# A SwiGLU kernel: two adjacent x rows per partition in one load, and strided PSUM copies

## The chip, the cores and the metric

The kernel runs on one core of one Trainium2 chip. The metric is the device time of one execution in microseconds (us), taken as the median over several runs. Besides the timed runs there is one profiled execution, from which all views of the trace come.

## The reference

x has 2048 rows of 640 elements; w_gate and w_up are 640 x 1536, w_down is 1536 x 640; all are bf16.

```python
B, S, D, F = 1, 2048, 640, 1536

def reference(x, w_gate, w_up, w_down):
    g = _silu(x @ w_gate)
    u = x @ w_up
    return (g * u) @ w_down
```

## The kernel before

The rows of x are worked off in four blocks of 512 (`S_BLK`). Everything contracts over the partitions, so x is needed turned: `xT` holds x with the 640 inner elements as 5 slices (`KD`) of 128 partitions and the 2048 rows as columns. The weights stay in SBUF whole: `wg_sb` and `wu_sb` by 5 slices, `wd_sb` by 12 chunks (`KF`).

For each block and each of the 12 chunks of F, TensorE makes a gate tile `pg` and an up tile `pu` (5 matmuls each, 128 x 512, in `proj`, line 193), ScalarE (ACT) takes the silu of `pg` into `sg` (line 214), and VectorE (DVE) multiplies `sg` with `pu` into `aT` (line 215). Then the block's output is made: 12 matmuls for the last 128 output columns (`po_t`, line 261), and four groups of 12 for the first 512 (`po_a`, line 291), with copies to SBUF and stores. The last four rows of x are worked out apart, on VectorE, as sums of products over turned weights (`row_dots`, line 147), between its other work.

How x comes into `xT`: rows 0 to 255 are loaded as they are, into `x_sb`, in two loads of 128 rows, one issued by SP and one by ACT (line 86), and turned by TensorE. Columns 256 to 511, 512 to 1023, 1024 to 1535 and 1536 to 2047 are turned by the DMA itself on the way in (`turn_x`, line 105), all issued by SP. The first of these is issued ahead of the up weights, the second behind all weight loads (`wd_sb`, line 125, is the last of them), the other two after block 0's outputs. Each gate slice `kd` of the first four chunks (`EARLY`) has its own load (line 115): slice 1 goes by ACT's queue, the others by SP's.

The start is written out in `head()`. TensorE runs 18 warm-up matmuls on a constant tile (`pw`, line 176), then for each of the two 128-row chunks of `x_sb` five transposes into PSUM tiles `pt` (line 185). Two copies per chunk carry them to `xT` (line 190): ACT takes slices 0 and 1, DVE slices 2 to 4. Then come 44 gate matmuls for the first four chunks (`proj_step`, line 193): slice 0 in two halves of 128 columns (4 + 4 matmuls), slices 1 to 4 over columns 0 to 255 (16), and slices 0 to 4 over columns 256 to 511 (20). After them come 20 up matmuls.

The order on SP, DVE, PE and ACT is the order of the program (`keep_order`, in `head` for PE and ACT). Which instruction waits for which is worked out by the framework from the memory that each reads and writes: a write that overlaps an earlier write of the same tile waits for it.

Of the kernel before, what the change touches and what calls it, by code (L numbers as in the profile page):

```python
# [10 lines left out]
def _body(  # L11
# [8 lines left out]
    nc = tc.nc  # L20
    P = nc.NUM_PARTITIONS
# [8 lines left out]
    x2 = x.rearrange("b s d -> (b s) d")  # L30
    out2 = out.rearrange("b s d -> (b s) d")

    KD = D // P
    KF = F // P
    S_BLK = 512
    NSB = S // S_BLK
    SUB = S_BLK // P
    HALF = S_BLK // 2
# [18 lines left out]
    x_sb = consts.tile([P, HALF // P, D], bf16)  # L57
    xT = consts.tile([P, KD, S], bf16)
    wg_sb = consts.tile([P, KD, F], bf16)
# [10 lines left out]

    make_identity(nc, ident[:])

    x_v = x2.rearrange("(c p) d -> p c d", p=P)
    xt_v = x2.rearrange("s (kd p) -> s kd p", p=P)
    wg_v = w_gate.rearrange("(kd p) f -> p kd f", p=P)
    wu_v = w_up.rearrange("(kd p) f -> p kd f", p=P)
# [2 lines left out]
    def wslice(a, b):  # L79
        return slice(a * P, b * P)  # L80

    def load_w(eng, dst, src, a, b):
        eng.dma_start(out=dst[:, :, wslice(a, b)], in_=src[:, :, wslice(a, b)])

    def load_x(eng, c0, c1):
        eng.dma_start(out=x_sb[:, c0:c1, :], in_=x_v[:, c0:c1, :])  # L86

    def issue_order(a, b):
        tc.add_manual_dep(
# [8 lines left out]
    def keep_order(engine):  # L98

        traced = [i for i in nc.cur_bb.bb.instructions if i.engine == engine]  # L100
        for a, b in zip(traced, traced[1:]):
            issue_order(a, b)
# [5 lines left out]
    silu_first = consts.tile([P, 1], f32)  # L108
    nc.vector.memset(ones[:], 1.0)  # L109

    load_x(nc.sync, 0, 1)
    load_x(nc.scalar, 1, 2)
    for kd in range(KD):
        eng = nc.scalar if kd == 1 else nc.sync
        eng.dma_start(
            out=wg_sb[:, kd, wslice(0, EARLY)], in_=wg_v[:, kd, wslice(0, EARLY)]
        )
# [11 lines left out]
    def turn_w(dst, src, f0, f1):  # L129
# [7 lines left out]
        out=x_row[:],  # L137
        in_=x2[S - T : S, :].rearrange("t d -> (t d)").partition_broadcast(P),
# [35 lines left out]
    def warm(n):  # L174
        for _ in range(n):
            nc.tensor.matmul(  # L176
                pw[:, 0:P], lhsT=ones[:], rhs=ones[:], start=True, stop=True
            )

    def transpose_chunk(c, parts):  # L180
        c_sl = slice(c * P, (c + 1) * P)
        for copy, tag, k0, k1 in parts:
            pt = psum.tile([P, k1 - k0, P], bf16, tag=tag, name="pt")
            for kd in range(k0, k1):
                nc.tensor.transpose(  # L185
                    out=pt[:, kd - k0, :],
                    in_=x_sb[:, c, kd * P : (kd + 1) * P],
                    identity=ident[:],
                )
            copy(out=xT[:, k0:k1, c_sl], in_=pt[:])  # L190

    def proj_step(ps, w_sb, fc, sb, c0, c1, kd):
        nc.tensor.matmul(  # L193
            ps[:, c0:c1],
            lhsT=w_sb[:, kd, fc * P : (fc + 1) * P],
            rhs=xT[:, kd, sb * S_BLK + c0 : sb * S_BLK + c1],
            start=(kd == 0 and c0 in (0, HALF)),
            stop=(kd == KD - 1),
        )

    def proj(ps, w_sb, fc, sb, c0, c1):
        for kd in range(KD):
            proj_step(ps, w_sb, fc, sb, c0, c1, kd)
# [6 lines left out]
    def gate(pg, pu, sb, fc, n_s):  # L210

        s0 = sb * S_BLK
        sg = work.tile([P, S_BLK], f32, name="sg")
        nc.scalar.activation(sg[:, 0:n_s], pg[:, 0:n_s], ACT.Silu)  # L214
        nc.vector.tensor_tensor(  # L215
            out=aT[:, fc, s0 : s0 + n_s], in0=sg[:, 0:n_s], in1=pu[:, 0:n_s], op=ALU.mult
        )

    def head():
        dve, act = nc.vector.tensor_copy, nc.scalar.copy  # L220
        split = [(act, "po_a", 0, 2), (dve, "po_b", 2, KD)]
        pgs = [
            psum.tile([P, S_BLK], f32, tag="gu", name="pg", bufs=4)
            for _ in range(EARLY)
        ]
        warm(N_WARM)
        for c in range(HALF // P):
            transpose_chunk(c, split)

        steps = [(0, 0, P), (0, P, HALF)]  # L230
        steps += [(kd, 0, HALF) for kd in range(1, KD)]
        steps += [(kd, HALF, S_BLK) for kd in range(KD)]
        for kd, c0, c1 in steps:
            for fc in range(EARLY):
                proj_step(pgs[fc], wg_sb, fc, 0, c0, c1, kd)

        for fc in range(EARLY):
            pu = psum.tile([P, S_BLK], f32, tag=("po_a", "po_b")[fc % 2], name="pu")
            proj(pu, wu_sb, fc, 0, 0, S_BLK)
            gate(pgs[fc], pu, 0, fc, S_BLK)  # L240
        keep_order(mybir.EngineType.PE)
        keep_order(mybir.EngineType.Activation)

    head()
    for sb in range(NSB):
        n_s = S_BLK if sb < NSB - 1 else S_BLK - T
# [13 lines left out]
        for kf in range(KF):  # L260
# [3 lines left out]
                rhs=aT[:, kf, sb * S_BLK : sb * S_BLK + n_t],  # L264
# [8 lines left out]
        for q in range(P // Q):  # L273
            nc.scalar.dma_start(
                out=out2[
                    sb * S_BLK : sb * S_BLK + n_t, DA + q * Q : DA + (q + 1) * Q
                ].rearrange("(i r) c -> r i c", r=Q),
                in_=ot_q[q * Q : (q + 1) * Q, :].rearrange("r (i c) -> r i c", c=Q),
            )

        for j in range(SUB):
# [6 lines left out]
            for c0, c1, tag in cols:  # L288
                po = psum.tile([P, c1 - c0], f32, tag=tag, name="po_a")
                for kf in range(KF):  # L290
# [3 lines left out]
                        rhs=wd_sb[:, kf, c0:c1],  # L294
# [8 lines left out]
                eng = nc.sync if c1 < D else nc.scalar  # L303
# [82 lines left out]
def kernel(tc, *args):  # L386
    _body(tc, *args)
    tc.close()
    tc.compile()
    _trim(tc.nc)  # L390
# [30 lines left out]
```

## Time and profile before

| what | value |
|---|---|
| median of 3 runs | 163.31 us (163.09 to 163.35) |
| span of the profiled execution, first to last instruction | 161.8 us |
| TensorE (PE) busy | 159.4 us, 99% of the span |
| VectorE (DVE) busy | 111.0 us, 69% |
| ScalarE (ACT) busy | 42.6 us, 26% |
| DMA moved | 15.86 MB |
| granted TensorE clock | 1.000 |

For the profiled execution the trace gives its span alone; the median of the timed runs is 1.5 us longer than that span.

How to read the views: PE is TensorE's matmuls, PEld its weight loads, SP the engine that issues most transfers; SPq and ACTq are instructions that an engine's sequencer handles, such as the issue of a transfer. A tile stands under its name in the program. `x44` is a count. "Idle before" is the time for which an engine stood still ahead of an instruction, and the arrow names what ended it. The span is also cut into 40 equal slices of 4.0 us, with a digit for the busy tenths in each. A transfer has an issue (the time that the issuing sequencer spends on it) and a landing (when all its data are in).

### The profile page before, as it was taken

Reading aid. Unit: us, or ns where it says so; the run is one execution under the profiler, and the core shown is the slowest. Engines: PE = TensorE matmul, PEld = TensorE weight load, DVE = VectorE, ACT = ScalarE, POOL = GpSimd, SP = SyncE. Lnnn points to the kernel's source line nnn. Section 1 sums busy time; section 2 is a strip of 40 time slices with the busy share of each in tenths; the row PEclk is TensorE's granted clock in tenths of the full one; section 3 lists DMA queues with packets and bytes.
Section 4 is the critical chain, followed back from the end, with each engine's and each line's share of the span. In section 5 each row is a group of like instructions: output and inputs, shape, how many; then the busy total and the mean of one; then the engine's idle time right before and its main releaser. Section 6 shows DMA issues by size and latency. Waiting matters only on the chain.

```text
span 161.8 us, 2142 instructions
## 1 busy us (share of the span) xinstructions
PE 159.4 (99%) x808; PEld 77.6 (48%) x808; DVE 111.0 (69%) x250; ACT 42.6 (26%) x74; POOL 0.6 (0%) x6
## 2 busy tenths in 40 slices
PE   8999999999999999999999999999999999999995
PEld 7854444444444444444444444444444444445454
DVE  2034223599569999989919999979964999993001
ACT  5051222112222222211222322221214222222121
POOL 1000000000000000000000000000000000000000
PEclk9999999999999999999999999999999999999999
DMA  6999999934189999003110000000321000000312
GB/s 212 231 351 349 361 248 231 222 75 91 34 192 159 235 236 184 4 0 34 65 65 0 0 4 2 0 0 3 62 67 34 0 0 0 0 0 4 48 41 73
DMA packets 41961, 15.86 MB, mean 98 GB/s; under 512 B 33504, under 2 KB 41824, under 8 KB 41952
## 3 DMA queue, kind: packets, MB, share of 16 engines
q1 hardware_dynamic: 33584, 14.93, 37.0%
q10 hardware_dynamic: 8368, 0.80, 3.5%
q8 instruction: 6, 0.10, 0.3%
q14 instruction: 3, 0.02, 0.1%
HBM read 6.88 MB, written 2.62 MB: 59 GB/s over the span
## 4 chain that ended last, share of the span: by engine, by line
PE 97%; DMA 2%; SPq 0%; DVE 0%; issue 0%
PE pg L193 32%; PE pu L193 32%; PE po_a L291 26%; PE po_t L261 6%; DMA wg_sb<-in_w_gate_dram 2%; SPq L86 0%; DVE ot_b L302 0%
## 5 line engine op out<-in xcount | busy, mean ns | idle before, releaser
L193 PE MATMUL pg<-xT,wg_sb 128*128 128x512 bf16 (+3 forms) x264 | 59.8, 363 | 0.1
L193 PE MATMUL pu<-xT,wu_sb 128*128 128x512 bf16 (+1 forms) x240 | 59.1, 379 | 0.0
L215 DVE TENSOR_TENSOR aT<-sg,pu 128x512 bf16<-128x512 f32 (+1 forms) x48 | 32.7, 682 | 32.3 <-PE pu L193 32.3
L214 ACT ACTIVATE sg<-pg 128x512 f32<-128x512 f32 (+1 forms) x48 | 28.4, 597 | 71.2 <-PE pg L193 67.4
L291 PE MATMUL po_a<-wd_sb,aT 128*128 128x512 bf16 (+4 forms) x228 | 42.8, 348 | 0.0
L147 DVE SCALAR_TENSOR_TENSOR prod<-wgT,x_row 128x640 f32<-128x640 bf16 x48 | 39.4, 821 | 1.5 <-DMA wgT<-in_w_gate_dram 0.4
L147 DVE SCALAR_TENSOR_TENSOR prod<-wuT,x_row 128x640 f32<-128x640 bf16 x48 | 39.4, 821 | 1.0
L193 PEld LDWEIGHTS <-wg_sb 128*128 128x128 bf16 x264 | 25.9, 100 | 26.8 <-DMA wg_sb<-in_w_gate_dram 0.4
L193 PEld LDWEIGHTS <-wu_sb 128*128 128x128 bf16 x240 | 23.4, 98 | 28.1 <-DMA wu_sb<-in_w_up_dram 0.3
L291 PEld LDWEIGHTS <-aT 128*128 128x128 bf16 x228 | 20.8, 98 | 21.7
L300 ACT CAST ot<-po_a 128x512 bf16<-128x512 f32 (+2 forms) x17 | 9.5, 559 | 31.8 <-PE po_a L291 20.2
L261 PE MATMUL po_t<-aT,wd_sb 128*128 128x512 bf16 (+1 forms) x48 | 10.4, 366 | 0.0
L261 PEld LDWEIGHTS <-wd_sb 128*128 128x128 bf16 x48 | 4.7, 98 | 5.1
L302 DVE CAST ot_b<-po_a 128x96 bf16<-128x96 f32 (+1 forms) x2 | 0.5, 240 | 9.7 <-PE po_a L291 9.6
L270 ACT CAST ot_t<-po_t 128x512 bf16<-128x512 f32 (+1 forms) x4 | 2.2, 559 | 11.6 <-PE po_t L261 11.6
L147 DVE DVE_READ_ACCUMULATOR prod<-wgT,x_row 128x1 f32 x48 | 3.9, 82 | 0.0
L147 DVE DVE_READ_ACCUMULATOR prod<-wuT,x_row 128x1 f32 x48 | 3.9, 82 | 0.0
L272 DVE STREAM_TRANSPOSE ot_q<-ot_t 128x512 bf16<-128x512 bf16 (+1 forms) x4 | 2.7, 676 | 1.7 <-ACT ot_t L270 1.7
L190 DVE COPY xT<-pt 128x384 bf16<-128x384 bf16 x2 | 0.7, 358 | 2.9 <-PE pt L185 2.9
L176 PE MATMUL pw<-ones 128*128 128x128 bf16 x18 | 2.1, 313 | 0.4 <-DVE ones L109 0.4
L176 PEld LDWEIGHTS <-ones 128*128 128x128 bf16 x18 | 1.8, 147 | 0.4 <-DVE ones L109 0.4
L119 ACT ACT_TABLE_LOAD x1 | 1.3, 1283 | 1.0 <-issue 1.0
(13 smaller groups left out, 4.7 us busy)
## 6 DMA issues: line engine op xcount, KB each, us to landing
wd_sb<-in_w_down_dram SPq DMA_DIRECT2D x1, 1920.0 KB, 13.0
out_dram<-ot SPq DMA_DIRECT2D x15, 128.0 KB, 1.7
wg_sb<-in_w_gate_dram SPq DMA_DIRECT2D x2, 640.0 KB, 7.9
wu_sb<-in_w_up_dram SPq DMA_DIRECT2D x2, 640.0 KB, 8.6
wu_sb<-in_w_up_dram SPq DMA_DIRECT2D x2, 320.0 KB, 4.7
x_row<-in_x_dram SPq DMA_DIRECT2D x1, 640.0 KB, 5.1
wg_sb<-in_w_gate_dram SPq DMA_DIRECT2D x4, 128.0 KB, 3.4
out_dram<-ot_q ACTq DMA_DIRECT2D x12, 32.0 KB, 1.9
```

What stands on the lines that cost most here:

```text
L119: nc.scalar.activation(silu_first[:], ones[:, 0:1], ACT.Silu)
L147: nc.vector.scalar_tensor_tensor(out=prod[:], in0=wT[:, fc, :], scalar=1.0, in1=x_row[:, t, :], op0=ALU.mult, op1=ALU.mult, accum_out=acc[ ...
L176: nc.tensor.matmul(pw[:, 0:P], lhsT=ones[:], rhs=ones[:], start=True, stop=True)
L190: copy(out=xT[:, k0:k1, c_sl], in_=pt[:])
L193: nc.tensor.matmul(ps[:, c0:c1], lhsT=w_sb[:, kd, fc * P : (fc + 1) * P], rhs=xT[:, kd, sb * S_BLK + c0 : sb * S_BLK + c1], start=(kd == 0 ...
L214: nc.scalar.activation(sg[:, 0:n_s], pg[:, 0:n_s], ACT.Silu)
L215: nc.vector.tensor_tensor(out=aT[:, fc, s0 : s0 + n_s], in0=sg[:, 0:n_s], in1=pu[:, 0:n_s], op=ALU.mult)
L261: nc.tensor.matmul(po_t[:], lhsT=wd_sb[:, kf, DA:D], rhs=aT[:, kf, sb * S_BLK : sb * S_BLK + n_t], start=(kf == 0), stop=(kf == KF - 1),)
L270: nc.scalar.copy(ot_t[:], po_t[:])
L272: nc.vector.transpose(out=ot_q[:], in_=ot_t[:])
L291: nc.tensor.matmul(po[:], lhsT=aT[:, kf, s0 : s0 + P], rhs=wd_sb[:, kf, c0:c1], start=(kf == 0), stop=(kf == KF - 1),)
L300: nc.scalar.copy(ot[:], po[:])
```

## The change

Rows 0 to 255 of x come in one load by SP. Partition p takes rows 2p and 2p+1, which lie next to each other in memory, instead of rows p and 128+p. The five transposes of "chunk" c therefore give the columns c, c+2, c+4 and so on up to 255, and the copies from PSUM write `xT` with a step of 2. The first eight gate matmuls, which begin when one chunk is there, read `xT` and write `pg` with a step of 2 as well. ACT's queue no longer has a load of x, and carries gate slice 0 in place of slice 1.

```diff
-    x_v = x2.rearrange("(c p) d -> p c d", p=P)
+    x_v = x2[0:HALF, :].rearrange("(p r) d -> p r d", r=2)
...
-    load_x(nc.sync, 0, 1)
-    load_x(nc.scalar, 1, 2)
+    nc.sync.dma_start(out=x_sb[:], in_=x_v)
     for kd in range(KD):
-        eng = nc.scalar if kd == 1 else nc.sync
+        eng = nc.scalar if kd == 0 else nc.sync
...
-            copy(out=xT[:, k0:k1, c_sl], in_=pt[:])
+            copy(out=xT[:, k0:k1, c:HALF:2], in_=pt[:])
...
-    def proj_step(ps, w_sb, fc, sb, c0, c1, kd):
+    def proj_step(ps, w_sb, fc, sb, c0, c1, kd, step=1):
         nc.tensor.matmul(
-            ps[:, c0:c1],
+            ps[:, c0:c1:step],
             lhsT=w_sb[:, kd, fc * P : (fc + 1) * P],
-            rhs=xT[:, kd, sb * S_BLK + c0 : sb * S_BLK + c1],
+            rhs=xT[:, kd, sb * S_BLK + c0 : sb * S_BLK + c1 : step],
...
-        steps = [(0, 0, P), (0, P, HALF)]
-        steps += [(kd, 0, HALF) for kd in range(1, KD)]
-        steps += [(kd, HALF, S_BLK) for kd in range(KD)]
-        for kd, c0, c1 in steps:
+        steps = [(0, 0, HALF, 2), (0, 1, HALF, 2)]
+        steps += [(kd, 0, HALF, 1) for kd in range(1, KD)]
+        steps += [(kd, HALF, S_BLK, 1) for kd in range(KD)]
+        for kd, c0, c1, step in steps:
             for fc in range(EARLY):
-                proj_step(pgs[fc], wg_sb, fc, 0, c0, c1, kd)
+                proj_step(pgs[fc], wg_sb, fc, 0, c0, c1, kd, step)
```

More of the change, by code (lines that the diff above doesn't have):

```diff
@@ L83, in load_w @@
         eng.dma_start(out=dst[:, :, wslice(a, b)], in_=src[:, :, wslice(a, b)])
-    def load_x(eng, c0, c1):
-        eng.dma_start(out=x_sb[:, c0:c1, :], in_=x_v[:, c0:c1, :])
     def issue_order(a, b):
@@ L180, in transpose_chunk @@
     def transpose_chunk(c, parts):
-        c_sl = slice(c * P, (c + 1) * P)
         for copy, tag, k0, k1 in parts:
```

## The prediction

> **What bounds the kernel now.** I read the page first: busy time by engine, and the chain of work that ended last.
>
> ```profile
> span 161.8 us, 2142 instructions
> PE 159.4 (99%) x808; PEld 77.6 (48%) x808; DVE 111.0 (69%) x250; ACT 42.6 (26%) x74; POOL 0.6 (0%) x6
> PE   8999999999999999999999999999999999999995
> PE 97%; DMA 2%; SPq 0%; DVE 0%; issue 0%
> ```
>
> TensorE is busy for 99% of the span and is 97% of the chain. Only its first and last slices fall below 9. So the time is a fixed train of matmuls plus what stands ahead of it and behind it; a delay of the train's start is a delay of the end, unless the train has holes that can take it up. The chain in order of time shows whether it has (start, length, what, count):
>
> ```profile
> 0.45 3.21 DMA wg_sb<-in_w_gate_dram
> 3.71 5.21 PE pg L193 x44
> 8.92 4.37 PE pu L193 x20
> 13.29 1.08 PE pg L193 x5
> 14.36 1.08 PE pu L193 x5
> ...
> 30.55 2.59 PE po_t L261 x12
> 33.14 10.36 PE po_a L291 x48
> 43.50 1.08 PE pg L193 x5
> ...
> 148.85 11.10 PE po_a L291 x84
> ```
>
> Each piece begins where the one before it ends: there are no holes from 3.71 us on. The change touches only what stands ahead of, and within, the piece of 44 gate matmuls. So the third view is the timeline of the first microseconds (start, length, engine, line, operation, tiles, count, idle before and its releaser):
>
> ```profile
> 0.00 0.39 SPq L86 DMA_DIRECT2D x_sb<-in_x_dram  x1
> 0.13 0.38 ACTq L86 DMA_DIRECT2D x_sb<-in_x_dram  x1
> 0.39 2.10 PE L176 MATMUL pw<-ones 128*128 128x128 bf16 x18 [0.39 <-DVE ones L109]
> 0.54 0.45 ACTq L115 DMA_DIRECT2D wg_sb<-in_w_gate_dram  x1
> 2.31 1.25 PE L185 MATMUL pt<-ident,x_sb 128*128 128x128 bf16 x10
> 2.33 1.91 SPq L105 DMA_TRANSPOSE xT<-in_x_dram  x1
> 2.74 0.37 ACT L190 COPY xT<-pt 128x256 bf16<-128x256 bf16 x1 [0.22 <-PE pt L185]
> 3.06 0.36 DVE L190 COPY xT<-pt 128x384 bf16<-128x384 bf16 x1 [2.73 <-PE pt L185]
> 3.71 4.93 PEld L193 LDWEIGHTS <-wg_sb 128*128 128x128 bf16 x44 [0.41 <-DMA wg_sb<-in_w_gate_dram]
> 8.79 4.00 PEld L193 LDWEIGHTS <-wu_sb 128*128 128x128 bf16 x20 [0.15 <-DMA wu_sb<-in_w_up_dram]
> 10.11 1.67 SPq L125 DMA_DIRECT2D wd_sb<-in_w_down_dram  x1
> 11.83 11.46 SPq L105 DMA_TRANSPOSE xT<-in_x_dram  x1
> ```
>
> The four copies out of PSUM (L190) wait for TensorE's transposes alone and have begun by 3.6 us. The last two rows matter most: the *second* turned load of x, which brings columns 512 to 1023 of xT, is issued at 11.83 us, behind every weight load, and holds the queue of SP for 11.46 us.
>
> **The change part by part.** *A new wait.* The edit that decides is the stride of the copies, and it shows in the program as built, whose list names the semaphores that each instruction waits for. Before, both first copies wait for PE alone. After, the rows are
>
> ```
> ACT  TensorCopy xT<-pt 128x2x128 [waits DMAHW6,PE]
> DVE  TensorCopy xT<-pt 128x3x128 [waits DMAHW6,PE]
> SP   DmaTransposeAnt xT<-in_x_dram 128x5x512 [waits DMAHW2,DVE]
> ```
>
> The wait on DMAHW6 is for a count of 32. Each load adds 16 to its semaphore, and DMAHW6 is raised by the first turned load (columns 256 to 511) and then by the second (512 to 1023), which itself waits for the first; so 32 means that the second has landed. No data asks for this. The copies write columns 0 to 255; but with a step of 2 the write is evidently taken as one range that reaches over its neighbours, and both turned loads stand earlier in the program. The third row is the same false overlap the other way round, for the third turned load; it is long satisfied when that load is issued after block 0, and costs nothing.
>
> When does the second turned load land? The view of the tile xT, cut to its issue, gives it from issue to landing:
>
> ```profile
> L105 SPq DMA_TRANSPOSE xT<-in_x_dram x1: 11462/11462/11462, 11.8 to 11.8; - x1
> DMA to landing us min/median/max: 13.5/13.5/13.5
> ```
>
> 11.83 + 13.5 = 25.3 us. Will it be so in the changed kernel? The queue of SP carries the same loads in the same order ahead of it, and the bytes over the 16 engines are the same: one x load of 320 KB where SP and ACT carried 160 KB each, and ACT keeps one gate slice. What holds it is traffic, by the windows (length, busy of PE, PEld, DVE, ACT, POOL, clock, DMA share, GB/s):
>
> ```profile
> 8.00:12.00 4.00, 4.00 (x24) 2.06 (x22) 1.37 (x2) 2.17 (x4) 0.00 (x0) 1.00 1.06 350
> 12.00:16.00 4.00, 4.00 (x20) 1.82 (x19) 1.82 (x3) 0.60 (x1) 0.00 (x0) 1.00 1.10 349
> 16.00:20.00 4.00, 4.00 (x20) 1.77 (x19) 1.05 (x3) 1.19 (x2) 0.00 (x0) 1.00 1.07 361
> ```
>
> From 8 to 20 us the DMA engines are full at about 350 GB/s, and no load of this stretch waits for a compute engine, so a stalled TensorE neither slows nor speeds them. I keep 25.3, with 0.4 us to each side: SP issues one x load instead of sharing it, and a 0.39 us issue is the size of what may shift.
>
> *What is queued behind the wait.* ACT: its second copy, then the silu of the first tiles. DVE: its second copy, then the products. TensorE: the 18 warm-up matmuls and ten transposes run as before and end near 4 us (the x load now comes whole, and a landing at up to 20 us is hidden). Then its first gate matmul waits for ACT's copy and, as TensorE runs in order, everything stands behind it for some 21 us.
>
> *The copy on the path.* ACT's first copy took 0.37 us and is now strided. No row shows a strided write: its bounds are 0.37 (no dearer) and 0.74 (half the pace). I take 0.37, since it moves the same number of elements, and add 0.1 for the two hand-overs (the first gate matmul at 3.71 came 0.05 after its load, 0.45 + 3.21 = 3.66). First gate matmul: 25.3 + 0.37 + 0.1 = 25.8 us. ACT's second copy and both of DVE's 0.36 us run beside the first eight matmuls and are hidden even at double length, as they are asked for 0.4 us and 1.7 us after the first.
>
> *The 44 gate matmuls.* They now restart after a gap. Two paces stand in the timeline of TensorE and in the view of line 193 (shortest, median and longest in ns, starts, forms):
>
> ```profile
> 3.71 1.42 PE L193 MATMUL pg<-xT,wg_sb 128*128 128x128 bf16 x10
> 6.57 2.34 PE L193 MATMUL pg<-xT,wg_sb 128*128 128x256 bf16 x20
> ```
>
> ```profile
> L193 PE MATMUL pg<-xT,wg_sb x44: 269/273/421, 3.7 to 8.6; 128*128 128x256 bf16 x36, 128*128 128x128 bf16 x8
> ```
>
> The 18 warm-up matmuls of 128 columns begin at 0.39 and the transposes at 2.31: 1.92/18 = 0.107 us from one to the next. The row at 6.57, less the last one's own length (0.27), gives 2.07/19 = 0.109 us for *twice* the columns. The first row is the timeline up to 4.9 us: ten gate matmuls had begun, eight of 128 columns and two of 256, and not yet the eleventh. 8 x 0.107 = 0.86 leaves over 0.33 us for those two, so they were still slow; at 0.21 each the pace changes at about 5.0 us, 4.6 us after the first matmul, although PEclk stands at 9 in the page and at 1.00 in the windows throughout. TensorE begins slowly after having been idle, then doubles.
>
> Does it begin slowly again after 21 us of idleness? The trace holds no such gap, so both ends are worked out. Fast: 8 x 0.054 + 36 x 0.109 = 4.4 us. Slow for 4.6 us again: 8 x 0.107 = 0.86, then 3.75/0.213 = 17.6, call it 18 at 0.213 = 3.83, and 18 at 0.109 = 1.96: 6.65 us. Slow throughout: 0.86 + 36 x 0.213 = 8.5 us. I take 6.65, as the start of the program is the nearest row: there too TensorE came from idleness. The eight strided matmuls might read or write at half pace; that is 0.86 us more of slow time, within which fewer later matmuls are slow, so some 0.4 us net; I take nothing and keep it for the range.
>
> [...]
>
> *The sum.* The up projections begin at 8.79 us now, and after them the train is whole. After: 25.8 + 6.65 = 32.45 us. The delay is 32.45 - 8.79 = 23.7 us. Span 161.8 + 23.7 = 185.5 us; the median of the runs, 163.31, stands 1.5 us over the profiled span, and I carry that: **187.0 us**.
>
> *Could later slack give it back?* By 32 us every weight of block 0 has landed, but TensorE did not wait for those. DVE and ACT are below their limits and shift along, as do the output stores and later turned loads, which SP issues behind block 0's outputs. At the end the order is the same. Nothing returns.
>
> *What the moved loads are worth.* The page's list of issues (KB each, us to landing) has:
>
> ```profile
> x_sb<-in_x_dram ACTq DMA_DIRECT2D x1, 160.0 KB, 2.6
> wg_sb<-in_w_gate_dram ACTq DMA_DIRECT2D x1, 128.0 KB, 3.3
> ```
>
> Gate slice 0 goes first on ACT's queue, at about 0.13 instead of 0.45 on SP's, and lands near 3.4 instead of 3.66; gate slice 1 goes to SP in its stead. All of it lies under the new wait. Even without that wait the up projections of block 0 stood 0.15 us idle for their own weights at 8.79, so an earlier start would have run into that load.
>
> **The rivals.**
>
> *The clock stays fast over the gap.* Restart at 25.8, 4.4 us, 30.2: delay 21.4, **184.7 us**. For it: PEclk shows no dip even in the slow start. Against: the pace at the start was half after idleness, whatever the digit says. Chance 0.06. *Slow to the end of the 44*: 34.3, delay 25.5, **188.8 us**. For it: how the slow stretch begins and ends is seen only once. Against: it lasted 4.6 us. Chance 0.06.
>
> *The wait ends with the first turned load.* If only columns 256 to 511 had to be in, the copies would start where that load lands:
>
> ```profile
> DMA to landing us min/median/max: 4.2/4.2/4.2
> ```
>
> 2.33 + 4.2 = 6.5 us; the gate matmuls then start near 7.0, 3.3 us late, and take at most the 5.1 us of before: about **166.6 us**. For it: it is the neighbour in memory and shares the semaphore. Against: the count is 32, not 16. Chance 0.02.
>
> *The wait never binds, and the change does what it says.* The place is the first copy; it decides if the load that it waits for is in by about 3 us, when the transposes allow the copy. Then the gate matmuls start by gate slice 0 (some 3.4 us) or by the ten transposes (all of x in by 0.13 + 2.6 = 2.7 as before, and 1.25: about 3.9), and the up projections still wait until their weights land just before 8.79: **163.2 us**, no slower than before. For it: the data are disjoint. Against: the load is issued at 11.83. Chance 0.02, half of it faster and half the same.
>
> **How the numbers follow.** Forecast as summed: 0.84, with its own range of 186.0 to 188.2 (0.4 for the landing, 0.4 for a dearer copy, 0.4 for strided matmuls, half of 1 us more or less of slow clock). With the two clock rivals the cases between 184.7 and 188.8 hold 0.96; I give these bounds, since they are the ends of the costs that no row shows. The measurement can tell about 0.2% from no change. Slower 0.98, same 0.01, faster 0.01.
>
> **What would show it.** In the profile after, the chain of waits should hold a DMA piece of xT up to 25.3 us, TensorE's digits should be near 0 from the second slice to the sixth, ACT's and DVE's L185 copies should start at 25.4, the first strided gate matmuls at 25.8, the first up projection near 32.4, and every later piece 23.7 us late with unchanged length. Slow pace at the restart shows as 0.107 us per 128 columns there. The forecast is wrong if the copies start before 20 us, or if the turned load at 11.83 lands elsewhere than 25.3.

## The result, and the profile after

| | before | after |
|---|---|---|
| median of 6 runs | 163.49 us (163.09 to 163.88) | 186.76 us (185.92 to 187.33) |
| ratio | | 1.1405, 95% interval 1.1369 to 1.1441 |
| span of the profiled execution | 161.8 us | 185.4 us |
| TensorE busy | 159.4 us, 99% | 160.5 us, 87% |

The change makes the kernel 14% slower. (The six runs before are the three of the table ahead of the prediction and three more.) The profiled execution of the changed kernel took 186.72 us, 1.3 us more than its span. Its page, with the same rows as before:

```profile
span 185.4 us, 2132 instructions
PE 160.5 (87%) x796; PEld 79.1 (43%) x808; DVE 111.4 (60%) x250; ACT 42.6 (23%) x74; POOL 0.6 (0%) x6
PE   7000049999999999999999999999999999999995
PE 85%; DMA 7%; SPq 6%; issue 1%; ACT 0%; DVE 0%; ACTq 0%
```

TensorE's work is nearly as long as it was; it now has a hole in the second to fifth slice (each is 4.6 us here), and the chain holds a good share of DMA and of SP's queue, 7% and 6% against 2% and 0%. The chain in order of time says which:

```profile
9.69 1.83 SPq L121
...
11.56 13.55 DMA xT<-in_x_dram
...
25.19 0.45 ACT xT L185
25.64 0.04 issue
25.69 6.84 PE pg L188 x44
...
36.84 1.08 PE pg L188 x5
```

The second turned load of x is issued at 11.56 us and lands at 25.11, ACT copies, TensorE starts. The chain before had only a gate slice ahead of TensorE. Who waited for whom (in total, times, longest):

```profile
DVE xT L185 <- DMA xT<-in_x_dram: 24.9, 1, 24.9
ACT xT L185 <- DMA xT<-in_x_dram: 23.1, 1, 23.1
PE pg L188 <- ACT xT L185: 21.4, 1, 21.4
```

One wait on each copying engine, and one of 21.4 us on TensorE behind them. The timeline of the start:

```profile
3.07 1.25 PE L180 MATMUL pt<-ident,x_sb 128*128 128x128 bf16 x10 [0.58 <-DMA x_sb<-in_x_dram]
...
25.19 0.75 ACT L185 COPY xT<-pt 128x256 bf16<-128x256 bf16 x2 [23.15 <-DMA xT<-in_x_dram]
25.21 1.05 DVE L185 COPY xT<-pt 128x384 bf16<-128x384 bf16 x2 [24.87 <-DMA xT<-in_x_dram]
25.69 6.84 PE L188 MATMUL pg<-xT,wg_sb 128*128 128x128 bf16 x44 [21.37 <-ACT xT L185]
...
32.36 4.48 PE L188 MATMUL pu<-xT,wu_sb 128*128 128x512 bf16 x19
```

The ten transposes were done near 4.3 us and their results lay in PSUM for 21 us. Less the last one's own length (0.31 us), they stand (1.25 - 0.31)/9 = 0.104 us apart for 128 columns: TensorE was still at its slow pace when the gap began. The first up matmul comes at 32.36 in place of 8.79: 23.6 us late, and the span is 23.6 us longer.

### The profile page after: what moved, and what is told of

Its sections match the earlier page's. It is cut to its first block, busy times and chain, and to the rows that moved or that the text cites. A ratio compares the mean times of both kernels' runs of the same rounds, so it can differ in the third digit from the quotient of the medians.

```text
span 185.4 us, 2132 instructions
## 1 busy us (share of the span) xinstructions
PE 160.5 (87%) x796; PEld 79.1 (43%) x808; DVE 111.4 (60%) x250; ACT 42.6 (23%) x74; POOL 0.6 (0%) x6
## 4 chain that ended last, share of the span: by engine, by line
PE 85%; DMA 7%; SPq 6%; issue 1%; ACT 0%; DVE 0%; ACTq 0%
PE pg L188 29%; PE pu L188 28%; PE po_a L286 23%; DMA xT<-in_x_dram 7%; PE po_t L256 5%; SPq L83 3%; SPq L121 1%; SPq L111 1%; SPq L102 1%; ACT xT L185 0%; SPq L108 0%; DVE ot_b L297 0%; ACTq L185 0%
## 5 line engine op out<-in xcount | busy, mean ns | idle before, releaser
L188 PE MATMUL pg<-xT,wg_sb 128*128 128x512 bf16 (+3 forms) x258 | 61.1, 373 | 21.7 <-ACT xT L185 21.4
L188 PEld LDWEIGHTS <-wg_sb 128*128 128x128 bf16 x264 | 27.4, 104 | 48.3 <-issue 21.5
L185 DVE COPY xT<-pt 128x384 bf16<-128x384 bf16 x2 | 1.1, 578 | 24.9 <-DMA xT<-in_x_dram 24.9
L185 ACT COPY xT<-pt 128x256 bf16<-128x256 bf16 x2 | 0.8, 446 | 23.1 <-DMA xT<-in_x_dram 23.1
```

The lines of the kernel that those rows point to most:

```text
L185: copy(out=xT[:, k0:k1, c:HALF:2], in_=pt[:])
L188: nc.tensor.matmul(ps[:, c0:c1:step], lhsT=w_sb[:, kd, fc * P : (fc + 1) * P], rhs=xT[:, kd, sb * S_BLK + c0 : sb * S_BLK + c1 : step], st ...
```

## The experiments

Each kernel was compared with runs of the kernel before on the same chip.

| run | time | ratio to before (95%) |
|---|---|---|
| e1, block 0's turned x in a tile of its own | 164.27 us | 1.005 (1.0022 to 1.0078) |
| e2, second turned load written behind the start | 168.54 us | 1.0286 (1.0264 to 1.0307) |
| e3, second turned load ahead of the down weights | 181.39 us | 1.1065 (1.1033 to 1.1096) |
| e4, gap filled with 350 matmuls | 189.59 us | 1.1574 (1.154 to 1.1607) |
| e5, e1 with plain first matmuls | 164.33 us | 1.0051 (1.0024 to 1.0078) |
| e6, e1 with x in two loads | 163.68 us | 1.0005 (0.9988 to 1.0021) |
| e7, gap filled with 400 matmuls | 187.45 us | 1.1453 (1.1429 to 1.1477) |
| e10, only the copies stepped | 187.24 us | 1.1426 (1.1394 to 1.1457) |
| e11, e6 with plain first matmuls | 163.66 us | 0.9991 (0.9976 to 1.0006) |

e8 and e9 ran once each (165.36 and 164.56 us). In both the share of gate slice 0 lies in other columns of the output, and only the pace of their matmuls is used.

### e1: the change without the false wait

```diff
-    xT = consts.tile([P, KD, S], bf16)
+    x0T = consts.tile([P, 2, KD, HALF], bf16)
+    xT = consts.tile([P, KD, S - S_BLK], bf16)
...
-            copy(out=xT[:, k0:k1, c:HALF:2], in_=pt[:])
+            copy(out=x0T[:, 0, k0:k1, c:HALF:2], in_=pt[:])
```

The first turned load writes `x0T[:, 1]`, and the full matmuls of block 0 read both halves at once (`x0T[:, :, kd, :]`).

> Everything of the change stays; only the place of block 0's turned x changes: columns 0-255 and 256-511 lie in two contiguous halves of a tile of their own, so that the stepped copies no longer wait for any turned load. If the false wait is nearly all of the loss (my theory): the copies start near 3.5 us, the first gate matmul near 4.2 (x in one load landed at 3.0, ten transposes after it), the first up matmul at 9.2 to 9.6 in place of 8.8, time 163.7 to 164.3. If the merged load, the stepped writes or the stepped matmuls cost several us by themselves: over 170. If the change without its wait gains: 163.2 or less.

164.27 us: without the wait, 0.5% is left of the 14%. Its timeline:

```profile
3.05 1.25 PE L185 MATMUL pt<-ident,x_sb 128*128 128x128 bf16 x10 [0.56 <-DMA x_sb<-in_x_dram]
3.48 0.98 ACT L190 COPY x0T<-pt 128x256 bf16<-128x256 bf16 x2 [1.43 <-PE pt L185]
4.09 5.88 PE L202 MATMUL pg<-x0T,wg_sb 128*128 128x128 bf16 x44
...
9.81 4.48 PE L202 MATMUL pu<-x0T,wu_sb 128*128 128x512 bf16 x20
```

The same stepped copies, matmuls and merged load: the copies follow the transposes, and the first up matmul comes at 9.81, a little later than forecast for this run. The first turned load still goes into the same tile as the copies, and it landed only at 6.8 us (issued at 2.34, 4.5 us to its landing). The copies at 3.48 did not wait for it, so against this load a contiguous half of the tile is enough.

### e2 and e3: which load is waited for, and how the time follows it

e2 changes only where the load stands in the program, not its place in SP's queue:

```diff
-    turn_x(S_BLK, 2 * S_BLK)
...
     head()
+    turn_x(S_BLK, 2 * S_BLK)
```

(The broadcast row and the first turned gate weights move with it, to keep the queue's order.) e3 moves the load one place up in the queue:

```diff
+    turn_x(S_BLK, 2 * S_BLK)
     nc.sync.dma_start(out=wd_sb[:], in_=wd_v)
...
-    turn_x(S_BLK, 2 * S_BLK)
```

> The changed kernel with the second turned load of x, the broadcast row and the turned gate weights written behind the start in the program; SP issues everything in the same order. The copies should then wait for the first turned load alone (landed at 7.0 us). If the second turned load is what was waited for: first gate matmul near 7.6; 44 gate matmuls in 4.8 us if the clock stays fast over 3.3 us of idleness, 6.7 if it falls, so a delay of 3.6 to 5.5 us: 167.1 to 169.0. If anything else held the copies: 186 to 187 as before.

> The changed kernel with the second turned load issued one place earlier, ahead of the down weights (1920 KB). By the theory the copies follow its landing: 17.5 us (the last up weights) and 2.2 us more, 19.7 in place of 25.1, so 5.4 us less: 181.4, copies at 19.8. A wait on the end of all weight loads would leave 186 to 187.

Both came out as forecast. In e2's timeline the copies start at the landing of the first turned load, and TensorE's 44 matmuls are slow after 2.77 us without work (14.17 - 7.44 = 6.73 us to the first up matmul, against 4.80 in e7 below):

```profile
3.42 1.25 PE L173 MATMUL pt<-ident,x_sb 128*128 128x128 bf16 x10 [0.93 <-DMA x_sb<-in_x_dram]
...
6.95 0.76 ACT L178 COPY xT<-pt 128x256 bf16<-128x256 bf16 x2 [4.90 <-DMA xT<-in_x_dram]
...
7.44 6.89 PE L181 MATMUL pg<-xT,wg_sb 128*128 128x128 bf16 x44 [2.77 <-ACT xT L178]
...
14.17 1.03 PE L181 MATMUL pu<-xT,wu_sb 128*128 128x512 bf16 x3
```

The ten transposes ahead of that gap are as slow as in the changed kernel (1.25 us for ten). So e2 does not show that the gap slowed TensorE down; it had not been fast yet. e4 and e7 below put that question.

In e3's chain the load starts at 9.88 and the copies at 19.71 (forecast 19.8):

```profile
9.88 9.76 DMA xT<-in_x_dram
...
19.71 0.45 ACT xT L185
20.17 0.04 issue
20.21 7.28 PE pg L188 x44
```

The landing came 5.5 us sooner than in the changed kernel, and the time fell by 186.76 - 181.39 = 5.4 us. So the copies wait for the last turned load of `xT` that stands ahead of them in the program, and the time follows its landing.

### e10: the copies' step alone

```diff
-        steps = [(0, 0, HALF, 2), (0, 1, HALF, 2)]
-        steps += [(kd, 0, HALF, 1) for kd in range(1, KD)]
+        steps = [(kd, 0, HALF, 1) for kd in range(KD)]
```

> The changed kernel with plain gate matmuls: four of 256 columns instead of eight stepped ones of 128; the copies keep their step. If the copies' step alone brings the wait: copies at 25.2 us again, and the gate matmuls only about 0.4 us shorter (0.85 us less of slow work, within a slow stretch that is as long), 186.3. If the stepped reads or writes of TensorE brought the wait: copies at 3.5 and about 164.

187.24 us. The chain:

```profile
11.61 13.54 DMA xT<-in_x_dram
...
25.23 0.76 ACT xT L185 x2
26.00 0.04 issue
26.04 7.39 PE pg L188 x40
```

The copies wait as in the changed kernel, so TensorE's stepped reads and writes are not what brings the wait. The small gain that was expected did not come. The plain matmuls need both of ACT's copies, so they start at 26.04 and not at 25.69, which the expectation left out; and the 40 took longer than the 44 (7.39 against 6.84), since the slow stretch after the restart was longer here: some 6 us by estimate, from 7.39 us against 40 x 0.109 = 4.4 at the fast pace, where the changed kernel had 3.8 us. What the stepped matmuls cost in the time can't be told from this run.

### e4 and e7: is the restart slow because TensorE was idle?

```diff
             transpose_chunk(c, split)
+        for _ in range(350):
+            nc.tensor.matmul(
+                pgs[0][:, 0:P], lhsT=ones[:], rhs=ones[:], start=True, stop=True
+            )
```

> The changed kernel with 350 more warm-up matmuls of 128 columns behind the transposes, which fill most of the gap (to about 24 us) and write a tile that is overwritten later. If idleness slowed the clock at the restart: the 44 gate matmuls take 8 x 0.107 + 36 x 0.109 = 4.8 us instead of 6.7, time 184.9, the strided ones at 0.107 us each (or 0.055 if the stride costs nothing). If the slow restart has another cause: 6.7 us and 186 to 187 as before.

> The kernel of e4 with 400 filling matmuls in place of 350, since 3 us of gap stayed there and the second turned load landed at 27.3. Filling to about 27.4 leaves under 1 us of idleness. If idleness makes the slow restart: the 44 gate matmuls take 4.4 to 4.8 us instead of 6.7 to 7.7, whenever they start (landing or end of filling, 25.7 to 28). If the slow pace comes from anything else at the restart: over 6 us again.

e4 missed: it was forecast at 184.9 us, or 186 to 187, and took 189.59. Its filling ended at 24.9 us, but the turned load landed at 27.3, and in the 3 us between TensorE fell back. Timeline of TensorE in e4:

```profile
14.81 10.10 PE L225 MATMUL pg<-ones 128*128 128x128 bf16 x178
27.88 7.83 PE L188 MATMUL pg<-xT,wg_sb 128*128 128x128 bf16 x44 [2.97 <-ACT xT L185]
```

and of e7, with 400 filling matmuls:

```profile
14.83 12.11 PE L225 MATMUL pg<-ones 128*128 128x128 bf16 x214
28.39 4.96 PE L188 MATMUL pg<-xT,wg_sb 128*128 128x128 bf16 x44 [1.45 <-ACT xT L185]
33.19 1.03 PE L188 MATMUL pu<-xT,wu_sb 128*128 128x512 bf16 x3
```

The filling runs at 10.10/178 = 0.057 us, the fast pace. After 2.97 us of idleness the 44 matmuls take 7.83 us, after 1.45 us they take 4.96. The granted clock, averaged over a run, tells the two apart in all four runs of each: 0.982 to 0.991 in e4, 1.000 in e7. So idleness makes a fast TensorE slow: 2.97 us were enough in e4, 1.45 us were not in e7. No run places the limit more closely than between these two. e7 is still no faster than the changed kernel, because the load that all wait for landed at 27.8 us there.

### e5, e6 and e11: the rest of 0.5%

e5 is e1 with e10's plain matmuls. e6 is e1 with the x load cut in two again, by row parity, and gate slice 1 on ACT's queue:

```diff
-    nc.sync.dma_start(out=x_sb[:], in_=x_v)
+    nc.sync.dma_start(out=x_sb[:, 0, :], in_=x_v[:, 0, :])
+    nc.scalar.dma_start(out=x_sb[:, 1, :], in_=x_v[:, 1, :])
     for kd in range(KD):
-        eng = nc.scalar if kd == 0 else nc.sync
+        eng = nc.scalar if kd == 1 else nc.sync
```

> The kernel of e1 with the eight stepped gate matmuls of 128 columns replaced by four plain ones of 256, which need both chunks. In e1 the eight stepped ones stood 0.213 us apart, as long as 256 columns at the slow pace. If the step costs that and no more: the gate matmuls start at 4.5 (second copy of ACT) and the first up matmul comes at 9.6 to 9.8 against 9.81, time 163.9 to 164.3. If the steps are the whole rest of the loss: first up matmul at 8.8 to 9.2 and 163.2 to 163.7.

> The kernel of e1 with rows 0-255 of x loaded again by two transfers, one on SP's queue (even rows) and one on ACT's (odd rows), and gate slice 1 on ACT's queue as before. If the merged load is 0.4 us of the rest (transposes at 3.05 instead of 2.31): transposes at 2.3 to 2.5, first gate matmul at 3.7, first up matmul at 9.3 to 9.5 against 9.81, time 163.7 to 164.0. If the one load costs nothing: 9.8 and 164.3 again.

> The kernel of e6 (x in two loads again) with the plain matmuls of e5: of the change, only adjacent rows and the stepped copies are left, without the false wait. By the terms: second copy of ACT ends near 4.0, first up matmul at 8.8 to 9.2, time 163.3 to 163.7, no difference from before that can be told. A gain would need the up weights, which landed at 8.7 to 9.0, to come sooner, and nothing here does that.

e5 gave 164.33 us against e1's 164.27: no difference, and in its profile the first up matmul came at 10.00, outside what was expected (9.6 to 9.8, or 8.8 to 9.2). e6 gave 163.68 us, which can't be told from before. Timeline of e6:

```profile
2.58 1.25 PE L186 MATMUL pt<-ident,x_sb 128*128 128x128 bf16 x10
3.02 0.98 ACT L191 COPY x0T<-pt 128x256 bf16<-128x256 bf16 x2 [0.49 <-PE pt L186]
...
3.63 5.72 PE L203 MATMUL pg<-x0T,wg_sb 128*128 128x128 bf16 x44
...
9.18 3.19 PE L203 MATMUL pu<-x0T,wu_sb 128*128 128x512 bf16 x14
```

With two loads the transposes start at 2.58 us, with one at 3.05; everything behind comes 0.5 to 0.6 us sooner. The one transfer of 320 KB keeps the first transposes waiting for all of it (in e1 it landed at 3.01 us), while two of 160 KB let the first chunk begin on its own (in the kernel before the transposes began at 2.31 us, and the second of the two landed at 0.13 + 2.6 = 2.7). e6 also gives gate slice 0 back to SP's queue, so this is the price of the load's form as a whole. e11, with the two loads and the plain matmuls, is at 163.66 us; no kernel of this series beats the one before. One thing stays open: single runs of e1 and e5, with one load, spread from 163.44 to 165.82 us, and those of e6 and e11, with two, only from 163.03 to 164.23. No run shows why.

### e8 and e9: what a step costs a matmul

Both are e1 with the step taken from one side of the eight first matmuls. e8 writes with a step and reads without, e9 the other way round:

```diff
-            rhs=x_cols(kd, sb, c0, c1, step),
+            rhs=x_cols(kd, sb, c0, c1, 1)
+            if step == 1
+            else x_cols(kd, sb, c0 * P, (c0 + 1) * P, 1),
```

```diff
-            ps[:, c0:c1:step],
+            ps[:, c0:c1] if step == 1 else ps[:, c0 * P : (c0 + 1) * P],
```

> The kernel of e1 in which the eight first gate matmuls write PSUM with a step of 2 but read xT without one (they then take other columns of x, so the output of gate slice 0 is mixed up). If the stepped PSUM write sets the 0.213 us of a matmul of 128 columns: 0.213 again. If the stepped read does: 0.107 at the slow pace.

> The counterpart of e8: the eight first gate matmuls read xT with a step of 2 and write PSUM without one (their results then lie in other columns, so the share of gate slice 0 is mixed up). e8's stepped writes stood 0.213 us apart at the slow pace. If the write alone sets that: 0.107 here at the slow pace or 0.055 at the fast one. If a stepped read costs as much: 0.213 again.

Groups of line 202 by shape (busy, mean ns of one, idle before), first of e8:

```profile
L202 PE MATMUL pg<-x0T,wg_sb 128*128 128x256 bf16 x36 | 5.1, 311 | 0.0
L202 PE MATMUL pg<-x0T,wg_sb 128*128 128x128 bf16 x8 | 1.9, 486 | 0.2 <-ACT x0T L190 0.2
```

then of e9:

```profile
L202 PE MATMUL pg<-x0T,wg_sb 128*128 128x256 bf16 x36 | 5.2, 314 | 0.0
L202 PE MATMUL pg<-x0T,wg_sb 128*128 128x128 bf16 x8 | 1.1, 309 | 0.0
```

Eight matmuls of 128 columns take 1.9 us with a stepped PSUM write (less the last one's 0.49: 1.4/7 = 0.20 each) and 1.1 us with a stepped read (0.8/7 = 0.11, the slow pace of the plain ones). The write is what costs: a stepped write of 128 columns takes 0.20 us, about as long as 256 columns in a row at the slow pace (0.21). e7 shows the same at the fast pace: from its first gate matmul to its first up matmul the 44 take 33.19 - 28.39 = 4.80 us, 0.109 each with the eight stepped ones among them. With those at the 0.057 us of the filling matmuls it would be 4.4.

## Why the prediction was right

*The wait.* The prediction's first step, that the stepped write is taken as one range over its neighbours and so waits for the second turned load, is what happened. e1 shows that this wait is nearly the whole loss, e10 that the copies' step brings it, e2 that it is the load's place in the program that counts, and e3 that the time follows the landing. How the framework compares the ranges was read from the lists of waits, not shown by a run.

*The landing.* Put at 25.3, it came at 25.11. Here the prediction had some luck. Its reason, that TensorE's work neither slows nor speeds the loads, is not shown: behind the same loads it landed at 27.3 and 27.8 us in e4 and e7, whose only edit is the filling matmuls, and that is far outside the 0.4 us that the prediction allowed.

*The copy.* Put at 0.37 with 0.1 for hand-overs. ACT's copy took 0.45 (row at 25.19 of the chain), with 0.13 around it, and the first gate matmul came at 25.69 for 25.8. DVE's copies lost more (0.578 us in place of 0.358), and were hidden as forecast. By shape, before and after:

```profile
L190 DVE COPY xT<-pt 128x384 bf16<-128x384 bf16 x2 | 0.7, 358 | 2.9 <-PE pt L185 2.9
```

```profile
L185 DVE COPY xT<-pt 128x384 bf16<-128x384 bf16 x2 | 1.1, 578 | 24.9 <-DMA xT<-in_x_dram 24.9
```

*The 44 matmuls.* Put at 6.65 us, they took 32.36 - 25.69 = 6.67. That this sum is right is luck: two of its terms were off and cancelled. The eight stepped matmuls, taken at 0.107 us each, stood 0.213 apart; the slow stretch, taken as 4.6 us, was shorter. TensorE's timeline up to 29.5 us, and from there on:

```profile
25.69 4.11 PE L188 MATMUL pg<-xT,wg_sb 128*128 128x128 bf16 x19 [21.37 <-ACT xT L185]
29.48 3.05 PE L188 MATMUL pg<-xT,wg_sb 128*128 128x256 bf16 x26
```

In the first row nineteen had begun, eight stepped and eleven of 256 columns. Less the last one's own length (0.27 us), they stand 3.84/18 = 0.213 us apart, all at the slow pace. In the second row it is 2.78/25 = 0.111, the fast one. So the slow stretch ended at about 29.5, after 3.8 us. Worked out from these rows, the stepped writes cost some 0.4 us net, the size that the prediction kept for them in its range; no run shows this in the time.

*The slow restart.* The prediction asked whether TensorE begins slowly *again* after the gap. The ten transposes of the changed kernel, 0.104 us apart, show that it had not yet been fast when the gap began: in the kernel before, the pace changed at about 5.0 us, and here TensorE stopped at 4.3. So the slow restart was forecast rightly, but the changed kernel alone does not show that idleness brings it back. e4 shows that, after long fast work: 0.057 us per filling matmul, then 2.97 us of idleness and 7.83 us for the 44.

*The sum.* The span was put at 185.5 us and is 185.4. The median was reached with 1.5 us on top. Where a run's time and span are both on record, as for the changed kernel (186.72 and 185.4), they lie 1.3 us apart, so some 0.2 us of the 1.5 was presumably a difference between two executions of the kernel before. The terms of the prediction's own range, taken together, would reach from 186.1 to 188.7 and not from 186.0 to 188.2; 186.76 lies in both. The 1 us more or less of slow clock in that range was the author's estimate, and no run shows it as a bound: the slow stretch, taken as 4.6 us, lasted 3.8 us here and some 6 us in e10 (an estimate from its 7.39 us for 40 matmuls).

*The rivals.* The fast restart is excluded by the slow pace in the row at 25.69 (0.213 us from one matmul to the next); it also had no fast pace to start from. The wait for the first turned load alone was forecast at 166.6 us. e2 built that case and took 168.54: its 44 matmuls took 14.17 - 7.44 = 6.73 us, where the rival allowed at most the 5.1 us of before. It left out that TensorE, stopped before it was fast, still had its slow stretch ahead, and that the stepped matmuls cost more. The case that the wait never binds was forecast at 163.2; e1 built it and took 164.27. The step that failed there is "all of x in by 0.13 + 2.6 = 2.7 as before": x in one load was in at 3.0 us, and the first chunk, which could be turned from 2.3 us on before, had to wait for all of it. And the 44 matmuls behind took 9.81 - 4.09 = 5.72 us in place of 5.08.

*Nothing was given back.* The pieces of the chain behind the start have the length that they had, 1.08 us for five matmuls, and come 23.6 us later, as in the row at 36.84 for the one at 13.29 before.

## What to carry to other kernels

Before a write into a shared tile gets a step, read in the built program what it waits for: a stepped range can be ordered behind the earlier transfers into that tile, as here behind both turned loads, and the price is the landing of the last of them (25.11 us in the changed kernel, 19.64 in e3). Where parts of a tile are filled by different means, give each part a contiguous place of its own (in e1 the copies began at 3.48 us). A transfer on the critical start is better cut so that the first consumer can begin on its piece, than merged into one (transposes at 2.58 us in e6, at 3.05 in e1).

## What the runs showed of the hardware

A matmul of 128 columns with a step of 2 on its PSUM side runs at half pace: 0.20 us in e8, against 0.107 for the warm-up matmuls of the kernel before, and in e7 0.109, the mean of its 44 with the eight stepped ones among them, against 0.057 for its filling ones. With a step on the side that it reads it does not (0.11 us, e9).

The length of TensorE's slow stretch varies from one profiled run to another: 3.8 us after the restart of the changed kernel, and in e10 7.39 us for 40 matmuls that would take 40 x 0.109 = 4.4 at the fast pace, so by estimate 3 us of loss and 6 us of slow work. At the start of the program too: the 36 matmuls of 256 columns took 5.1 us in e8 and 5.2 in e9, against 4.4 before. This spread, 0.8 us at the start of the program, is larger than the 0.4 us or so that the stepped writes cost by the estimate above, so e5 and e10 could not price them in the time.

The granted clock does not always show it. It stands at 1.00 in the changed kernel where the matmuls were slow (0.213 us apart), and at 0.50 in e4, which took 7.83 us for its 44 (windows: length, busy of PE, PEld, DVE, ACT, POOL, clock, DMA share, GB/s). After:

```profile
24.00:28.00 4.00, 2.31 (x12) 2.13 (x12) 1.05 (x2) 0.75 (x2) 0.00 (x0) 1.00 1.20 228
```

e4:

```profile
28.00:32.00 4.00, 4.00 (x20) 3.27 (x19) 0.45 (x1) 0.13 (x1) 0.00 (x0) 0.50 1.03 205
```

The second turned load landed at 25.1 us while TensorE stood still, and at 27.3 and 27.8 while it ran the filling matmuls. But it landed at 25.3 with TensorE busy in the kernel before and at 26.5 in e1. What moves it was not settled.
